# Spectral filter and gated convolution: the two relayouts of a 3200-point transform moved from DRAM passes to 32x32 block transposes

## The chip, the cores and the metric

The kernel runs on one core of one Trainium2 chip. The metric is the device time of one execution in microseconds, as the median of several runs. A profile of one execution is read beside it.

The core has five engines that each work through a queue of their own in order: TensorE (matmuls, PE in the profile, with PEld for loading its stationary operand), VectorE (DVE), ScalarE (ACT), GpSimd (POOL) and SyncE (SP), which here only issues DMAs. Semaphores order the engines among each other.

## The reference

For each of 8 batch elements and 256 channels, a sequence of 3200 samples goes through a real Fourier transform, is multiplied by a complex filter, and goes back. The result feeds a gated unit: a causal convolution of five taps per channel gives the gate, a 256x256 product gives the value, and a second product gives the output.

```python
X = np.fft.rfft(x, axis=1)                    # x: (8, 3200, 256)
Y = X * (filt_r + 1j * filt_i)[None, :, :]
x = np.fft.irfft(Y, n=3200, axis=1).astype(np.float32)
for k in range(5):
    gate_pre += conv_w[k][None, None, :] * xp[:, k:k + S, :]
gate = 1.0 / (1.0 + np.exp(-gate_pre))
return (gate * (x @ w_val)) @ w_out
```

## The kernel before

The transform is split in two stages. A sample index is n = 25 a + r, with a from 0 to 127 and r from 0 to 24 (`L = 128`, `R = 25`). Stage 1 transforms over a, stage 2 over r; the inverse goes the other way. Each stage is a matmul with a table of cosines and sines that the kernel makes at its start.

Every batch element passes through these functions, most of them seven times, one call for each chunk:

- `load_x` (L82): GpSimd issues the load of a chunk of x and its cast to bf16.
- `s1` (L298): stage 1, matmuls of 512 columns with `cf_t`; VectorE copies the PSUM tile to `so` (L310), and SyncE writes it to the DRAM scratch `dscr` (L312).
- `load_t` (L316): SyncE reads `dscr` back as `tt` with another layout (L326), five lines of 25 values to the 125 partitions. This is the first relayout.
- `s2` (L332): stage 2, four matmuls of 256 columns for each of 13 groups (L340 to L346). ScalarE copies PSUM to `xs` (L349); VectorE multiplies by the filter's real part (`za`, L354) and its imaginary part (`zb`, L358) and adds (`z`, L360).
- `inva` (L364): the inverse of stage 2, again four matmuls for each group (L376, L378). ScalarE copies to `u` (L381), and SyncE writes it to the DRAM scratch `escr` (L392).
- `load_v` (L394): SyncE reads `escr` back as `vt`. This is the second relayout.
- `invb` (L403): the inverse of stage 1, with the data as the stationary operand and `ci_t` as the moving one (L413). ScalarE scales it into `yt` (L415), where a row holds one channel and the free dimensions are r and the long index. GpSimd copies four halo rows (L422).
- `conv` (L424): the five taps as 20 matmuls of 64x64 with diagonal tables `dg_t` (L431); ScalarE's sigmoid makes the gate `gt` (L436).
- `val` (L441): four matmuls with `wv_t` (L448); VectorE multiplies the gate with the PSUM tile into `gv` (L453).
- `outp` (L459): eight matmuls with `wo_t` (L465); even chunks are copied to `o` by VectorE (L470), odd ones by ScalarE (L473), and SyncE writes them out (L475).

All PSUM tiles come from one pool of four (L70), each 128 x 1024 float32, and are taken in program order. The order around is written out as one loop over chunk steps (L491), in which each function has a lag in chunks: stage 2 runs nine steps behind stage 1, the inverse of stage 1 ten further. The x loads run seven steps, one batch element, ahead.

Of the kernel before, what the change touches and what calls it, by code (L numbers as in the profile page):

```python
# [11 lines left out]
I32 = mybir.dt.int32  # L12
AF = mybir.ActivationFunctionType
ALU = mybir.AluOpType

PI = math.pi
# [3 lines left out]


L = 128
R = 25
NG = 13
GL = 5
NQ = 2 * NG
P2 = GL * R

PCH = [(0, 4), (4, 4), (8, 4), (12, 3), (15, 3), (18, 3), (21, 4)]
ICH = [PCH[-1]] + PCH[:-1]  # L30
GCH = [(0, 2), (2, 2), (4, 2), (6, 2), (8, 2), (10, 2), (12, 1)]
NCH = 7
# [3 lines left out]
def kernel(  # L36
# [14 lines left out]
    assert D == 256 and S == L * R and K == 5  # L51
# [3 lines left out]
    cf_t = cpool.tile([128, 130], FP16, name="cf_t")  # L55
    ci_t = cpool.tile([128, 128], FP16, name="ci_t")
    wc_t = cpool.tile([128, NG, 128], FP16, name="wc_t")
    ws_t = cpool.tile([128, NG, 128], FP16, name="ws_t")
    wsn_t = cpool.tile([128, NG, 128], FP16, name="wsn_t")
    vc_t = cpool.tile([128, NG, 128], FP16, name="vc_t")  # L60
    vs_t = cpool.tile([128, NG, 128], FP16, name="vs_t")
    vsn_t = cpool.tile([128, NG, 128], FP16, name="vsn_t")
# [5 lines left out]
    b_npi = cpool.tile([128, 1], FP32, name="b_npi")  # L68

    pp = ctx.enter_context(tc.tile_pool(name="ps", bufs=4, space=bass.MemoryType.PSUM))  # L70
    dpool = ctx.enter_context(tc.tile_pool(name="scr", bufs=2, space=bass.MemoryType.DRAM))
    xpool = ctx.enter_context(tc.tile_pool(name="xin", bufs=10))
    spool = ctx.enter_context(tc.tile_pool(name="s1o", bufs=4))
    tpool = ctx.enter_context(tc.tile_pool(name="s2i", bufs=8))
# [4 lines left out]

    xts = {}  # L80

    def load_x(b, j):  # L82
        p0, np_ = PCH[j]
        xt = xpool.tile([128, 4, D], BF16, name="xt")
        src = x[b].rearrange("(a r) d -> a r d", r=R)[:, p0:p0 + np_, :]
        nc.gpsimd.dma_start(out=xt[:, 0:np_, :], in_=src)  # L86
        xts[(b, j)] = xt

    for j in range(NCH):
        load_x(0, j)  # L90


    with tc.tile_pool(name="gen", bufs=1) as g1, \
         tc.tile_pool(name="gen2", bufs=2) as g2, \
         tc.tile_pool(name="genf", bufs=1) as gf:

        def floormod(src_ap, divisor):
            shp = list(src_ap.shape)
            divi = g2.tile(shp, I32, name=f"fm_i{shp[1]}")
            bak = g2.tile(shp, FP32, name=f"fm_b{shp[1]}")  # L100
# [390 lines left out]
    for G in range(total):  # L491
        c = at(G, -NCH)
        if c is not None:
            load_x(*c)
# [57 lines left out]
```

## Time and profile before

| | |
|---|---|
| median of 3 runs | 387.34 us (385.9 to 387.5) |
| the profiled execution, first to last instruction | 385.9 us |
| instructions | 8019 |
| HBM read and written | 56.59 MB and 52.43 MB |
| x loads (GpSimd's queue), share of the 16 DMA engines' time | 28.1% |
| all other transfers (SyncE's queue) | 62.5% |
| first and last start of the convolution's matmuls | 101.3 and 374.8 us |

In the profile's slices, each digit stands for a fortieth of the span and gives the busy share in tenths. The chain of waits follows the work that ended last back to the start and says what it was held by at each step. The groups give, for a line and a shape, the busy time, the mean duration of one instruction, and the idle time of the engine before it with what ended that idle time. The windows give the engines' busy time in a stretch of the execution.

### The profile page before, as it was taken

What the parts mean: (1) busy time and instruction counts of PE and PEld (TensorE: products, weight loads), DVE (VectorE), ACT (ScalarE), POOL (GpSimd) and SP (SyncE); (2) the same over time, 40 slices, a digit from 0 to 9 for tenths busy, and PEclk for the clock granted to TensorE, in tenths of its full rate; (3) what the DMA queues carried; (4) which work ended last, traced back from release to release, by engine and by line L of the source; (5) the groups of instructions that cost most, each with busy time, mean ns of one, the idle gap of its engine ahead of it and who ended that gap; (6) DMA issues with size and microseconds to landing.
All of it is one profiled execution on the core that took longest, in us unless ns stands there. A gap on an engine that the chain in (4) does not pass through costs nothing.

```text
span 385.9 us, 8019 instructions
## 1 busy us (share of the span) xinstructions
PE 312.3 (81%) x3089; PEld 206.9 (54%) x3089; DVE 284.9 (74%) x462; ACT 229.1 (59%) x255; POOL 64.2 (17%) x131
## 2 busy tenths in 40 slices
PE   0230477475899999999997999899999999999992
PEld 0100145253656756766675666566676677666661
DVE  4999958553858887888787789678977677765554
ACT  1100235334976777677765776677677878867660
POOL 8797211112110211021102011100010001001000
PEclk9999998766989999999999999999999999999998
DMA  7999999999999999999999999989595968449343
GB/s 124 144 162 190 216 257 251 231 250 280 179 250 249 311 286 273 263 282 332 274 301 303 286 269 298 285 299 319 201 351 170 304 223 299 136 142 323 141 191 152
DMA packets 94118, 94.53 MB, mean 245 GB/s; under 512 B 10102, under 2 KB 74624, under 8 KB 94080
## 3 DMA queue, kind: packets, MB, share of 16 engines
q1 hardware_dynamic: 80064, 78.98, 62.5%
q0 software_dynamic: 14016, 15.04, 28.1%
q8 instruction: 24, 0.39, 0.4%
q14 instruction: 14, 0.11, 0.1%
HBM read 56.59 MB, written 52.43 MB: 282 GB/s over the span
## 4 chain that ended last, share of the span: by engine, by line
PE 44%; DVE 20%; DMA 19%; SPq 8%; issue 4%; ACT 2%; POOL 1%; DVEq 0%; ACTq 0%; POOLq 0%
PE ps L431 12%; PE ps L448 7%; DMA escr<-u 6%; PE ps L465 6%; DVE so L310 6%; DMA vt<-escr 5%; SPq L326 5%; PE ps L413 5%; DMA dscr<-so 4%; PE ps L376 3%; DVE gv L453 3%; DMA tt<-dscr 3%; PE ps L378 3%; PE ps L307 3%; DVE za L354 2%
## 5 line engine op out<-in xcount | busy, mean ns | idle before, releaser
L415 ACT ACTIVATE yt<-ps 128x1024 bf16<-128x1024 f32 (+1 forms) x56 | 52.1, 931 | 44.3 <-PE ps L413 44.2
L453 DVE TENSOR_TENSOR gv<-ps,gt 128x1024 bf16<-128x1024 f32 (+1 forms) x56 | 61.9, 1104 | 18.7 <-PE ps L448 13.7
L310 DVE CAST so<-ps 128x1024 bf16<-128x1024 f32 (+1 forms) x56 | 61.5, 1103 | 19.0 <-PE ps L307 15.9
L354 DVE TENSOR_TENSOR za<-xs,fr_t 125x1024 bf16<-125x1024 bf16 (+1 forms) x56 | 37.3, 665 | 50.5 <-ACT xs L349 50.3
L381 ACT ACTIVATE u<-ps 125x1024 bf16<-125x1024 f32 (+1 forms) x56 | 53.9, 963 | 24.4 <-PE ps L378 21.6
L431 PE MATMUL ps<-yt,dg_t 64*64 64x512 bf16 (+1 forms) x1120 | 65.7, 361 | 0.8
L349 ACT ACTIVATE xs<-ps 125x1024 bf16<-125x1024 f32 (+1 forms) x56 | 54.0, 965 | 19.6 <-PE ps L346 18.4
L436 ACT ACTIVATE gt<-ps 128x1024 bf16<-128x1024 f32 (+1 forms) x56 | 52.4, 935 | 9.1 <-PE ps L431 5.9
L86 POOL DMA_DIRECT2D xt<-in_x_dram x56 | 30.2, 569 | 153.0 <-PE ps L307 146.5
L307 PE MATMUL ps<-xt,cf_t 128*128 128x512 bf16 x112 | 36.9, 421 | 22.4 <-DVE so L310 11.4
L465 PE MATMUL ps<-wo_t,gv 128*128 128x256 bf16 x400 | 52.8, 273 | 0.9 <-DVE gv L453 0.9
L448 PE MATMUL ps<-yt,wv_t 128*128 128x512 bf16 (+1 forms) x224 | 52.6, 357 | 0.0
L465 PEld LDWEIGHTS <-gv 128*128 128x128 bf16 x400 | 39.1, 98 | 14.9 <-DVE gv L453 1.2
L413 PE MATMUL ps<-ci_t,vt 128*128 128x128 f16 x400 | 31.9, 221 | 13.3 <-DMA vt<-escr 9.6
L431 PEld LDWEIGHTS <-dg_t 64*64 64x64 bf16 x1120 | 30.1, 106 | 23.2 <-issue 10.1
L340 PE MATMUL ps<-tt,wc_t 125*128 125x256 bf16 x104 | 30.1, 289 | 12.9 <-DMA tt<-dscr 10.6
L470 DVE COPY o<-ps 128x1024 f32<-128x1024 f32 (+1 forms) x32 | 36.7, 1148 | 1.1 <-PE ps L465 1.1
L360 DVE TENSOR_TENSOR z<-za,zb 125x1024 bf16<-125x1024 bf16 (+1 forms) x56 | 36.4, 650 | 1.3
L413 PEld LDWEIGHTS <-vt 128*128 128x128 bf16 x400 | 27.0, 98 | 17.9 <-DMA vt<-escr 10.7
L358 DVE TENSOR_TENSOR zb<-xs,fm_t 125x1024 bf16<-125x1024 bf16 (+1 forms) x56 | 36.2, 646 | 0.0
L376 PE MATMUL ps<-z,vc_t 125*128 125x256 bf16 x104 | 30.0, 289 | 6.9 <-DVE z L360 6.9
L307 PEld LDWEIGHTS <-cf_t 128*128 128x128 f16 x112 | 9.2, 108 | 41.7 <-issue 28.2
(109 smaller groups left out, 386.6 us busy)
## 6 DMA issues: line engine op xcount, KB each, us to landing
out_dram<-o SPq DMA_DIRECT2D x32, 512.0 KB
tt<-dscr SPq DMA_DIRECT2D x48, 256.0 KB
escr<-u SPq DMA_DIRECT2D x48, 224.0 KB
out_dram<-o SPq DMA_DIRECT2D x24, 384.0 KB
xt<-in_x_dram POOLq DMA_DIRECT2D x32, 256.0 KB, 6.5
dscr<-so SPq DMA_DIRECT2D x32, 256.0 KB
vt<-escr SPq DMA_DIRECT2D x32, 256.0 KB
xt<-in_x_dram POOLq DMA_DIRECT2D x24, 192.0 KB, 5.7
```

Source lines behind the costliest of these rows:

```text
L307: nc.tensor.matmul(ps[:, a * D:e * D], lhsT=cf_t[:, 0:128], rhs=xt[:, a:e, :], start=True, stop=True)
L310: nc.vector.tensor_copy(so[:, 0:np_, :].rearrange("p a d -> p (a d)"), ps[:, 0:np_ * D])
L349: nc.scalar.activation(xs[0:P2, 0:ng, :, :].rearrange("p g c d -> p (g c d)"), ps[0:P2, 0:ng * 512], AF.Copy)
L354: nc.vector.tensor_tensor(za[0:P2, 0:ng], xs[0:P2, 0:ng], fr_t[0:P2, g0:g0 + ng, :].unsqueeze(2).to_broadcast((P2, ng, 2, D)), op=ALU.mult)
L381: nc.scalar.activation(u[0:P2, 0:2 * ng, :].rearrange("p q d -> p (q d)"), ps[0:P2, 0:ng * 512], AF.Copy)
L413: nc.tensor.matmul(ps[:, o:o + L], lhsT=v[:, a, 128 * dh:128 * dh + 128], rhs=ci_t[:, :], start=True, stop=True)
L415: nc.scalar.activation(y[:, :, H + p0:H + p0 + np_, :].rearrange("p h a n -> p h (a n)"), ps[:, :].rearrange("p (h n) -> p h n", h=2)[:, : ...
L431: nc.tensor.matmul(ps[64 * dh:64 * dh + 64, 512 * r:512 * r + np_ * L], lhsT=dg_t[rows, dh, k, :], rhs=y[rows, dh, p0 + k:p0 + k + np_, :] ...
L436: nc.scalar.activation(g[:, :, 0:np_ * L], ps[:, :].rearrange("p (h n) -> p h n", h=2)[:, :, 0:np_ * L], AF.Sigmoid)
L448: nc.tensor.matmul(ps[:, 512 * eh:512 * eh + np_ * L], lhsT=wv_t[:, dh, 128 * eh:128 * eh + 128], rhs=y[:, dh, H + p0:H + p0 + np_, :], st ...
L453: nc.vector.tensor_tensor(gv[:, :, 0:np_ * L], ps[:, :].rearrange("p (h n) -> p h n", h=2)[:, :, 0:np_ * L], g[:, :, 0:np_ * L], op=ALU.mult)
L465: nc.tensor.matmul(ps[:, D * a:D * a + D], lhsT=gv[:, eh, L * a:L * a + L], rhs=wo_t[:, eh, :], start=(eh == 0), stop=(eh == 1))
```

## The change

The sample index is split differently, n = 32 a + r, with a from 0 to 99 and r from 0 to 31 (`NI = 100`, `NR = 32`). Both relayouts stay in the core. Stage 1's output lies in one large tile `sbig` of a batch element, as 128 channel pairs x 32 values x 2 channels in each partition. VectorE transposes it in blocks of 32x32 words of four bytes, a word being a pair of channels in bf16, into `tbig`. The same is done from `ubig` to `vbig` between the two inverse stages. There are one `sbig`, one `tbig`, one `ubig` and two `vbig`.

```diff
-L = 128
-R = 25
+NI = 100
+NR = 32
-    dpool = ctx.enter_context(tc.tile_pool(name="scr", bufs=2, space=bass.MemoryType.DRAM))
-    xpool = ctx.enter_context(tc.tile_pool(name="xin", bufs=10))
+    xpool = ctx.enter_context(tc.tile_pool(name="xin", bufs=8))
+    sbig = [bigp.tile([128, 128, NR, 2], BF16, name=f"sb{n}") for n in range(1)]
+    tbig = [bigp.tile([128, 128, NR, 2], BF16, name=f"tb{n}") for n in range(1)]
+    ubig = [bigp.tile([128, 128, NR, 2], BF16, name=f"ub{n}") for n in range(1)]
+    vbig = [bigp.tile([128, 128, NR, 2], BF16, name=f"vb{n}") for n in range(2)]
+    def words(t):
+        return t[...].rearrange("p d q l -> p (d q l)").bitcast(U32)
     def s1(b, j):
+        for a in range(2):
+            nc.tensor.matmul(ps[:, 512 * a:512 * a + 512], lhsT=cf_t[0:NI, :],
+                             rhs=xt[0:NI, 2 * a:2 * a + 2, :], start=True, stop=True)
+        nc.scalar.activation(s[:, :, 4 * j:4 * j + 4, :],
+                             ps[:, :].rearrange("p (r d l) -> p d r l", r=4, l=2), AF.Copy)
-        nc.vector.tensor_copy(so[:, 0:np_, :].rearrange("p a d -> p (a d)"),
-                              ps[:, 0:np_ * D])
-        nc.sync.dma_start(
-            out=dscr[0:128 * R, :].rearrange("(i r) d -> i r d", r=R)[:, p0:p0 + np_, :],
-            in_=so[:, 0:np_, :])
+    def tr(dst, src, part):
+        n = 1024
+        nc.vector.transpose(out=words(dst)[:, n * part:n * part + n],
+                            in_=words(src)[:, n * part:n * part + n])
+    def tr1(b):
+        for part in range(4):
+            tr(tbig[b % len(tbig)], sbig[b % len(sbig)], part)
+    def tr2(b):
+        for part in range(4):
+            tr(vbig[b % len(vbig)], ubig[b % len(ubig)], part)
     def s2(b, m):
+            for co in range(2):
+                for h in range(2):
+                    t = 4 * m + 2 * a + h
+                    nc.tensor.matmul(
+                        ps[64 * h:64 * h + 64, 512 * a + D * co:512 * a + D * co + D],
+                        lhsT=wf_t[:, t, co].rearrange("p b k -> p (b k)"),
+                        rhs=tt[:, :, place(t), :], start=True, stop=True)
-        nc.vector.tensor_tensor(z[0:P2, 0:ng], za[0:P2, 0:ng], zb[0:P2, 0:ng],
-                                op=ALU.add)
+        nc.gpsimd.tensor_tensor(za[:, 0:ng], za[:, 0:ng], zb[:, 0:ng], op=ALU.add)
     def inva(b, m):
+            for c in range(2):
+                for h in range(2):
+                    rows = slice(64 * h, 64 * h + 64)
+                    nc.tensor.matmul(
+                        ps[:, 512 * h + D * a:512 * h + D * a + D],
+                        lhsT=wi_t[rows, 2 * m + a, c].rearrange("p b e r -> p (b e r)"),
+                        rhs=z[rows, a, c, :], start=(c == 0), stop=(c == 1))
+            nc.scalar.activation(u[:, :, 4 * m:4 * m + 4, :],
+                                 ps[:, :].rearrange("p (q d l) -> p d q l", q=4, l=2),
+                                 AF.Copy)
     def invb(b, j):
+                nc.tensor.matmul(ps[:, o:o + NI], lhsT=v[:, :, r0 + a, dh],
+                                 rhs=ci_t[:, :], start=True, stop=True)
     def outp(b, c):
-        if j % 2 == 0:
...
+        nc.vector.tensor_copy(o[:, 0:nq, :].rearrange("p a d -> p (a d)"), ps[:, 0:nq * D])
```

`load_t` and `load_v` are gone. Stage 1 has eight chunks for each batch element instead of seven. The convolution, the values and the outputs are cut along the long index: six chunks of 512 columns, which cover 16 values of a for all 32 values of r, and a seventh of 128. The moving operand of the convolution and of the values is then read as 16 neighbouring elements at a time.

The tables are smaller, and their making is rewritten: fewer VectorE instructions, each over 1664 elements, and three sines on ScalarE (`cf_t`, `wf_t` in two halves, `si`), of which `si` follows from `xi`. On VectorE the order that results puts the product of the filter's imaginary part and its sign (`fm_t`, two instructions) between the two halves of `xi`.

The loop over chunk steps is replaced by a list with due times, sorted once; the due times fix the order in which the work is issued:

```diff
+    work = []
+    for b in range(B):
+        for j in range(8):
+            if b + 1 < B:
+                work.append((b + 0.1 * j - 0.05, load_x, (b + 1, j)))
+            work.append((b + 0.1 * j, s1, (b, j)))
+        work.append((b + 0.85, tr1, (b,)))
+        for m in range(NCH):
+            work.append((b + 1.0 + 0.1 * m, s2, (b, m)))
+            work.append((b + 1.15 + 0.1 * m, inva, (b, m)))
+            work.append((b + 2.0 + 0.06 * m, invb, (b, m)))
+            work.append((b + 2.5 + 0.13 * m, conv, (b, m)))
+            work.append((b + 2.57 + 0.13 * m, val, (b, m)))
+            work.append((b + 2.7 + 0.13 * m, outp, (b, m)))
+        work.append((b + 1.9, tr2, (b,)))
+    for _, f, args in sorted(work, key=lambda w: w[0]):
+        f(*args)
```

## The prediction

> **What bounds the kernel now.** I read the busy table, the slices, the chain, then windows of one batch each.
>
> ```profile
> span 385.9 us, 8019 instructions
> PE 312.3 (81%) x3089; PEld 206.9 (54%) x3089; DVE 284.9 (74%) x462; ACT 229.1 (59%) x255; POOL 64.2 (17%) x131
> DMA  7999999999999999999999999989595968449343
> PE 44%; DVE 20%; DMA 19%; SPq 8%; issue 4%; ACT 2%; POOL 1%; DVEq 0%; ACTq 0%; POOLq 0%
> ```
>
> The DMA engines are full until slice 27 (about 260 us). The chain's DMA and SPq shares (27%) are the four DRAM passes, yet most of the chain is TensorE and VectorE. The windows' columns are length, then busy time of PE, PEld, DVE, ACT, POOL, then clock, DMA share and GB/s.
>
> ```profile
> 182.00:223.00 41.00, 37.58 (x390) 25.47 (x388) 32.01 (x41) 28.58 (x32) 5.01 (x10) 1.00 1.02 294
> 305.00:346.00 41.00, 41.00 (x459) 28.30 (x456) 29.54 (x38) 32.01 (x37) 1.29 (x3) 1.00 0.63 206
> ```
>
> In the middle DMA (1.02) and TensorE (37.6 of 41) are both full; later, with DMA down to 0.63, TensorE is busy for all 41 us. In the chain the first convolution of a batch recurs at 106.9, 145.8, 184.7, 225.2 and 265.1 us: a batch takes 39.6 us. So removing DRAM traffic alone gains little: a gain needs TensorE relieved too, and nothing put in its place.
>
> **Durations.** Columns: busy us, mean ns, idle before.
>
> ```profile
> L349 ACT ACTIVATE xs<-ps 125x1024 bf16<-125x1024 f32 x48 | 49.2, 1026 | 19.6 <-PE ps L346 18.4 <-DVE gv L453 0.4
> L453 DVE TENSOR_TENSOR gv<-ps,gt 128x1024 bf16<-128x1024 f32 x32 | 39.0, 1220 | 10.2 <-PE ps L448 5.6 <-ACT gt L436 4.5
> L470 DVE COPY o<-ps 128x1024 f32<-128x1024 f32 x24 | 29.2, 1215 | 1.1 <-PE ps L465 1.1
> L422 POOL COPY yt<-yt 128x508 bf16<-128x508 bf16 x16 | 9.3, 610 | 91.6 <-ACT yt L415 91.6
> L234 DVE TENSOR_SCALAR fm_t<-fi_t,sg 125x3328 bf16<-125x3328 bf16 x1 | 1.9, 1930 | 0.0
> ```
>
> Neighbours overlap, so what an engine pays is the distance between starts; the timeline (start, duration) shows it:
>
> ```profile
> 264.58 1.02 ACT L415 ACTIVATE yt<-ps 128x1024 bf16<-128x1024 f32 x1
> 265.50 0.59 ACT L349 ACTIVATE xs<-ps 125x512 bf16<-125x512 f32 x1
> 273.80 1.22 DVE L310 CAST so<-ps 128x1024 bf16<-128x1024 f32 x1
> 274.93 1.22 DVE L453 TENSOR_TENSOR gv<-ps,gt 128x1024 bf16<-128x1024 f32 x1
> 270.63 1.27 PE L431 MATMUL ps<-yt,dg_t 64*64 64x512 bf16 x20
> 271.84 0.60 PE L307 MATMUL ps<-xt,cf_t 128*128 128x512 bf16 x2
> ```
>
> ScalarE pays 0.92 us for 1024 columns (0.5 for 512, 0.74 for 800), VectorE 1.13 from PSUM and 0.61 for one of za, zb. Twenty 64-row, 64-column matmuls of 512 columns take 1.21 us, against 20 x 0.217 = 4.3 one after another: four tiles run at once.
>
> **The change, part by part (per batch).** *DMA.* The passes dscr, tt, escr and vt go with all SP issues but the output's. Of 94.5 MB some 41 stay, so DMA leaves the bound.
>
> *TensorE.* s1 has 16 matmuls of 512 columns: 3.5 us (2.8 before). s2 and inva keep 52 x 256 columns each, but two halves of the array work in pairs. By the four-tile row the pairs run together: 26 x 0.109 = 2.8 us each instead of 5.7; if not, 5.7. invb 64 x 100 columns at the L413 rate, 0.45 ns a column, about 3; convolution 7.5, val 5.5, outp 5.4. Sum 31 us, 36 without pairing. s2 and invb read every 64th element of a partition; no row here has that, bounded by nothing and by twice their matmul time (+6). I take nothing: TensorE then has 15 us of slack in the period below, which covers it; without that slack it would cost those 6.
>
> *ScalarE.* It gains the eight s1 evictions (8 x 0.92 = 7.4) and loses its three output copies. Per batch: s1 7.4, xs 6.0, u 6.0, y 5.8, gates 5.8: 31 us. s1 and u now scatter runs of eight elements; bounds 0.92 (xs row) and twice that. I take 0.92, the row of the same size.
>
> *VectorE.* It loses the so casts and z adds, takes all output copies, and gains eight transposes of 128x1024 words of four bytes. Bounds for one: 0.6 us (L234 does 3328 elements in 1.93 us, so 1024 in 0.6) and 2.26 (two passes of the copy row). I take 1.13, one pass of it: eight are 9.0 us. With za, zb 8.0, gv 7.1, o 7.1: 31 us. [...]
>
> *GpSimd.* The z add moves there. The copy row's pair takes 1.16 us for 2 x 508 elements, 1.14 ns each for one input; two inputs double it: 2.4 us an add (bounds 1.2 and, as twice that again, 4.8). Seven are about 16 us, and eight x loads of 0.53 us share the queue: 20 us, or 38 at the upper bound, under the period either way. GpSimd also holds VectorE up; here a copy pair meets a za:
>
> ```profile
> 209.07 1.16 POOL L422 COPY yt<-yt 128x508 bf16<-128x508 bf16 x2 [5.81 <-ACT yt L415]
> 209.96 0.82 DVE L354 TENSOR_TENSOR za<-xs,fr_t 125x1024 bf16<-125x1024 bf16 x1 [2.63 <-ACT xs L349]
> ```
>
> That za ends at 210.78, 0.55 us after the copies, and takes 0.82 instead of 0.69. [...]
>
> *Setup.* In the changed order all eight s1 evictions of batch 0 stand behind the activation of si, which needs xi, whose second half stands behind fm_t on VectorE, which needs the last filter load. GpSimd's first 8 loads and index work end near 12 us; 16 filter loads at 0.72 each (17.4 us for 24 before) bring it to 24; landing takes 3.8 (row of fi_t): 27.8. Then fm_t 2 x 1.9, the rest of xi, wrapping and copies 4.3, si 1.6: 37.6. Eight evictions 7.4 and four transposes 4.5: first s2 at 49.5 us (before, the first za is at 48.2).
>
> **The period.** Every transpose needs all 128 channels: tr1 waits for all eight s1 of the next batch, tr2 for all seven u, and with one buffer each the next s2, s1 and invb wait for them. On VectorE the order at the end of a batch is tr1 x3, o, gv, tr1, tr2 x4: 8 x 1.13 + 2 x 1.13 = 11.3 us. Behind it stands invb(0), first in TensorE's queue, and on ScalarE its eviction stands before all others; ScalarE has only two gates meanwhile. Then comes the window from the last transpose to the s1(7) eviction. ScalarE alone needs 0.6 + 28.7 us for it. I walked the four queues through it, each instruction starting at the latest of its queue, its input and its PSUM turn (four, in order). ScalarE loses about 5 us more: it waits 0.9 for xs(1) and 0.6 for y(2) (PSUM turns held by o and gv, which VectorE reaches only after the transposes), 0.6 for gate 0, 0.4 for u(5) (its add), 1.3 for s1(7), the rest in pieces under 0.5. s1(7) ends at 34.1, VectorE starts the transposes at 35.0, the next period at 46.3 us.
>
> The sum: first s2 49.5. Batch 0 through stage 2: 22 evictions 19.4, fill 4.9 (s2, za, zb, add, inva), eight transposes 9.0: 83. Second phase, three gates fewer: 43, so 126. Five full periods 231.5: 357.5. Last stage 2 without s1 and tr1: 46.3 - 7.4 - 4.5 = 34.4: 392. Rest: invb 2.8, eight full chunks at 2.93 (conv 1.19, val and outp 0.87 each), two small at 0.8, last gv, outp, copy and DMA 5.6 (before, the DMA took 4.5): 34. Total **426 us**, on the profile's terms; that execution's span of 385.9 lies 0.4% under the median 387.34 of runs 385.9 to 387.5, so nothing is added.
>
> **Rivals.** A, the forecast: two transposes at each batch's end that nothing covers, a period of 46.3; own range 405 to 450. For it: the dependence is structural and the buffers single. Against it: the walk rests on rows of other operations.
>
> B, not slower: ScalarE runs back to back in the window, because evictions free PSUM before TensorE asks. Place: last transpose to s1(7). Price: period 0.6 + 28.7 + 11.3 + 0.1 = 40.7, 5.6 less in some 7.2 periods, so 426 - 40 = 386 us; transposes below 1.13 take it under the time before. It decides below 40.9. For it: in the old window 305:346 TensorE kept 41 of 41. Against it: ScalarE was busy 32 of 41 there.
>
> C, slower still: scattered evictions cost more. Fifteen a batch; each 0.1 us more is 1.5 per period, 11 in all. At 0.3 more, 459 us. It decides from 0.2. Against it: the runs are as wide as a copy needs; no row tells.
>
> D, transposes in two passes: 8 x 1.13 more per period, about 7.8 periods: 426 + 70 = 496 us.
>
> **Chances and range.** A 0.50, B 0.26, C 0.16, D 0.08. About 0.5% is what a measurement of this kernel can tell from no change. B gives 0.22 for faster and 0.04 for same; 0.02 of A's and C's neighbourhood goes to same as well: faster 0.22, same 0.06, slower 0.72. The range must reach B's middle and most of C and D: 376 to 488.
>
> **What would show it.** Right: a transpose row near 1.1 to 1.2 us; ScalarE idle 8 to 10 us per batch until y(0), released through transposes; DMA share under 0.6; s2 and inva at half their time; a period of 45 to 48; first transposes near 45 us. Wrong: a period near 40 with ScalarE over 85% busy (B); s1 and u rows above 1.2 us (C); a transpose near 2.3 us (D); s2 pairs in series, which would put TensorE at 36 us and lengthen the window.

## The result, and the profile after

The changed kernel takes **476.36 us** (median of 3 runs, 474.74 to 477.2) against 387.34 before: 1.232 times the time before, 95% interval 1.225 to 1.239. The forecast was 426. The profiled execution has a span of 473.0 us, 3.4 under the median.

From its page, the lines that answer to those shown of before: the span, the busy table, the slices of TensorE, of its clock and of the DMA engines, and the chain by engine.

```profile
span 473.0 us, 7824 instructions
...
PE 346.1 (73%) x3218; PEld 186.6 (39%) x3218; DVE 294.7 (62%) x346; ACT 268.8 (57%) x294; POOL 179.3 (38%) x206
...
PE   0004356288969994999499949995999779769991
...
PEclk9999997589979999999999999998799989899997
DMA  7864342223434563546354544554222323224454
...
PE 42%; DVE 26%; POOL 10%; ACT 9%; issue 7%; DMA 3%; DVEq 0%; POOLq 0%; ACTq 0%
```

The transfers are gone as announced: behind the first three slices the DMA row lies at 2 to 6, where it held 9s before, and SP's queue leaves the chain. But TensorE's row is not full either. It shows 9s and then a 4 or 5, once a batch. TensorE is busy for 34 us longer than before (346.1 against 312.3), although two of its stages were to run at half their time.

One period in the middle, from one batch's last transpose to the next one's. The columns are those of the windows of before:

```profile
283.50:331.60 48.10, 41.73 (x402) 22.81 (x402) 32.69 (x37) 32.31 (x36) 19.57 (x18) 0.93 0.51 103
```

TensorE 41.7 of 48.1 us, VectorE 32.7, ScalarE 32.3, GpSimd 19.6. The forecast had TensorE at 31, VectorE and ScalarE at 31 each and GpSimd at 20. Three of the four lie within 2 us of it; TensorE is 11 us off. The groups (busy us, mean ns of one, then the idle time before them and its releaser) show where:

```profile
L299 POOL TENSOR_TENSOR za<-za,zb 128x1024 bf16<-128x1024 bf16 (+1 forms) x56 | 111.9, 1998 | 78.7 <-DVE zb L297 77.9
...
L260 ACT ACTIVATE sb<-ps 128x1024 bf16<-128x1024 f32 x64 | 65.1, 1033 | 10.0 <-PE ps L258 5.8
L334 PEld LDWEIGHTS <-vb 128*128 128x128 bf16 x512 | 52.0, 205 | 45.8 <-DVE vb L265 34.1
...
L284 PE MATMUL ps<-tb,wf_t 128*64 128x256 bf16 x416 | 59.0, 416 | 8.6 <-DVE tb L265 7.5
...
L316 ACT ACTIVATE ub<-ps 128x1024 bf16<-128x1024 f32 x48 | 49.4, 1029 | 13.7 <-PE ps L311 13.6
...
L392 PEld LDWEIGHTS <-gv 128*128 128x128 bf16 x400 | 36.4, 99 | 39.6 <-DVE gv L380 29.0
...
L265 DVE STREAM_TRANSPOSE tb<-sb 128x1024 uint32<-128x1024 uint32 x32 | 37.6, 1217 | 10.3 <-ACT sb L260 10.2
```

Loading 128 x 128 weights takes 205 ns where they come from `vbig` and 99 where they come from `gv`. The scattered evictions of ScalarE (L260, L316) cost 1.03 us, no more than the plain ones of before (1026 ns). A transpose costs 1.22 us.

The timeline at the end of a batch (start, duration, and in brackets the idle time before and its releaser):

```profile
272.07 3.50 DVE L265 STREAM_TRANSPOSE tb<-sb 128x1024 uint32<-128x1024 uint32 x3
...
275.49 1.19 DVE L395 COPY o<-ps 128x1024 f32<-128x1024 f32 x1
...
276.60 1.21 DVE L380 TENSOR_TENSOR gv<-ps,gt 128x1024 bf16<-128x1024 f32 x1
277.73 1.22 DVE L265 STREAM_TRANSPOSE tb<-sb 128x1024 uint32<-128x1024 uint32 x1
...
277.87 1.05 PE L392 MATMUL ps<-wo_t,gv 128*128 128x256 bf16 x8 [2.22 <-DVE gv L380]
...
278.75 1.04 PE L375 MATMUL ps<-yt,wv_t 128*128 128x512 bf16 x4
278.88 4.58 DVE L265 STREAM_TRANSPOSE vb<-ub 128x1024 uint32<-128x1024 uint32 x4
283.38 1.18 DVE L395 COPY o<-ps 128x1024 f32<-128x1024 f32 x1
...
283.52 0.95 PE L334 MATMUL ps<-ci_t,vb 128*128 128x100 f16 x8 [3.72 <-DVE vb L265]
...
284.49 1.21 DVE L380 TENSOR_TENSOR gv<-ps,gt 128x1024 bf16<-128x1024 f32 x1
284.57 0.84 ACT L336 ACTIVATE yt<-ps 128x800 bf16<-128x800 f32 x1 [7.84 <-PE ps L334]
```

This is the block that the forecast described: from 272.07 to 283.46 us VectorE has eight transposes, one o copy and one gv. TensorE still finds work in the first part of it, then waits 2.2 and 3.7 us, and ScalarE waits 7.8 us for the first `yt`.

With the ends of the tr2 blocks as marks, the sum of the forecast stands against the trace like this:

| stretch | forecast | measured | off by |
|---|---|---|---|
| to the end of the first tr1 | 49.5 | 55.4 | +5.9 |
| first phase, to the first tr2's end | 33.5 | 39.6 | +6.1 |
| second phase | 43 | 43.0 | 0 |
| five periods | 231.5 (46.3 each) | 242.8 (48.55) | +11.3 |
| last stage-2 phase | 34.4 | 44.9 | +10.5 |
| rest | 34 | 47.2 | +13.2 |
| sum | 426 | 473.0 | +47.0 |

Three of these stretches can be read in single lines. ScalarE at the start, the table `si` and then the eight s1 evictions:

```profile
37.63 1.59 ACT L173 ACTIVATE si<-xi 128x1664 f16<-128x1664 f32 x1 [16.79 <-DVE xi L86]
43.33 7.44 ACT L260 ACTIVATE sb<-ps 128x1024 bf16<-128x1024 f32 x8 [4.10 <-DVE dg_t L226]
```

The eight evictions take 7.44 us as forecast, but they begin 4.1 us after `si` ends. `sbig` lies in the memory in which the tables were made, so the first write into it waits for VectorE's last table instruction, a `dg_t`. `si` itself is 1.6 us late: it ends at 39.2 us and not at 37.6, because `fm_t` starts on VectorE at 29.55 us and not at 27.8. The loads of `fi_t` took 5.5 us to land in this profile, where the forecast had 3.8.

In the first phase, on TensorE, VectorE and GpSimd:

```profile
74.78 0.69 DVE L297 TENSOR_TENSOR zb<-xs,fm_t 128x1024 bf16<-128x1024 bf16 x1
...
76.66 0.55 POOL L70 DMA_DIRECT2D xt<-in_x_dram  x1 [1.87 <-PE ps L258]
...
77.05 2.87 DVE L293 TENSOR_TENSOR za<-xs,fr_t 128x1024 bf16<-128x1024 bf16 x1 [1.58 <-ACT xs L289]
77.23 2.13 POOL L299 TENSOR_TENSOR za<-za,zb 128x1024 bf16<-128x1024 bf16 x1
79.41 1.03 PE L311 MATMUL ps<-za,wi_t 64*128 64x256 bf16 x8 [3.04 <-POOL za L299]
```

The zb of one chunk ends at 75.47, but its add starts only at 77.23: a load of x stands ahead of it in GpSimd's queue and waits for s1. Then the next chunk's za, which needs 0.69 us alone, takes 2.87 and ends 0.56 us after the add. TensorE waits 3.04 us for the add.

In the rest, when only gating and output are left:

```profile
451.81 1.05 PE L392 MATMUL ps<-wo_t,gv 128*128 128x256 bf16 x8 [0.32 <-DVE gv L380]
...
452.69 1.05 PE L375 MATMUL ps<-yt,wv_t 128*128 128x512 bf16 x4
452.89 1.23 DVE L395 COPY o<-ps 128x1024 f32<-128x1024 f32 x1 [1.14 <-PE ps L392]
...
454.03 1.21 DVE L380 TENSOR_TENSOR gv<-ps,gt 128x1024 bf16<-128x1024 f32 x1
...
455.30 1.05 PE L392 MATMUL ps<-wo_t,gv 128*128 128x256 bf16 x8 [0.31 <-DVE gv L380]
```

From one outp to the next it takes 3.49 us. outp ends, o is copied, gv follows on the same engine, and the next outp waits for it. The forecast had added TensorE's three pieces, 2.93.

### The profile page after: what moved, and what is told of

It is laid out like the page before. It is cut to its first block, busy times and chain, and to the rows that moved or that the text cites. A ratio compares the mean times of both kernels' runs of the same rounds, so it can differ in the third digit from the quotient of the medians.

```text
span 473.0 us, 7824 instructions
## 1 busy us (share of the span) xinstructions
PE 346.1 (73%) x3218; PEld 186.6 (39%) x3218; DVE 294.7 (62%) x346; ACT 268.8 (57%) x294; POOL 179.3 (38%) x206
## 4 chain that ended last, share of the span: by engine, by line
PE 42%; DVE 26%; POOL 10%; ACT 9%; issue 7%; DMA 3%; DVEq 0%; POOLq 0%; ACTq 0%
PE ps L284 8%; PE ps L334 8%; PE ps L357 7%; DVE vb L265 7%; PE ps L392 6%; POOL za L299 6%; DVE tb L265 5%; DVE gv L380 4%; DVE o L395 4%; PE ps L311 4%; PE ps L375 4%; PE ps L258 4%; ACT ub L316 3%; ACT xs L289 2%; ACT sb L260 2%
## 5 line engine op out<-in xcount | busy, mean ns | idle before, releaser
L299 POOL TENSOR_TENSOR za<-za,zb 128x1024 bf16<-128x1024 bf16 (+1 forms) x56 | 111.9, 1998 | 78.7 <-DVE zb L297 77.9
L336 ACT ACTIVATE yt<-ps 128x1000 bf16<-128x1000 f32 (+1 forms) x56 | 52.7, 941 | 71.7 <-PE ps L334 71.7
L293 DVE TENSOR_TENSOR za<-xs,fr_t 128x1024 bf16<-128x1024 bf16 (+1 forms) x56 | 47.5, 847 | 72.8 <-ACT xs L289 72.2
L395 DVE COPY o<-ps 128x1024 f32<-128x1024 f32 (+1 forms) x56 | 61.5, 1099 | 48.9 <-PE ps L392 48.9
L334 PE MATMUL ps<-ci_t,vb 128*128 128x100 f16 x512 | 55.4, 257 | 30.6 <-DVE vb L265 29.8
L260 ACT ACTIVATE sb<-ps 128x1024 bf16<-128x1024 f32 x64 | 65.1, 1033 | 10.0 <-PE ps L258 5.8
L334 PEld LDWEIGHTS <-vb 128*128 128x128 bf16 x512 | 52.0, 205 | 45.8 <-DVE vb L265 34.1
L289 ACT ACTIVATE xs<-ps 128x1024 bf16<-128x1024 f32 (+1 forms) x56 | 54.4, 971 | 23.8 <-PE ps L284 19.0
L284 PE MATMUL ps<-tb,wf_t 128*64 128x256 bf16 x416 | 59.0, 416 | 8.6 <-DVE tb L265 7.5
L316 ACT ACTIVATE ub<-ps 128x1024 bf16<-128x1024 f32 x48 | 49.4, 1029 | 13.7 <-PE ps L311 13.6
L392 PEld LDWEIGHTS <-gv 128*128 128x128 bf16 x400 | 36.4, 99 | 39.6 <-DVE gv L380 29.0
L258 PE MATMUL ps<-xt,cf_t 100*128 100x512 bf16 x128 | 46.8, 460 | 6.3 <-ACT sb L260 4.9
L265 DVE STREAM_TRANSPOSE tb<-sb 128x1024 uint32<-128x1024 uint32 x32 | 37.6, 1217 | 10.3 <-ACT sb L260 10.2
```

Of the source, the lines that this page charges most:

```text
L258: nc.tensor.matmul(ps[:, 512 * a:512 * a + 512], lhsT=cf_t[0:NI, :], rhs=xt[0:NI, 2 * a:2 * a + 2, :], start=True, stop=True)
L260: nc.scalar.activation(s[:, :, 4 * j:4 * j + 4, :], ps[:, :].rearrange("p (r d l) -> p d r l", r=4, l=2), AF.Copy)
L265: nc.vector.transpose(out=words(dst)[:, n * part:n * part + n], in_=words(src)[:, n * part:n * part + n])
L284: nc.tensor.matmul(ps[64 * h:64 * h + 64, 512 * a + D * co:512 * a + D * co + D], lhsT=wf_t[:, t, co].rearrange("p b k -> p (b k)"), rhs=t ...
L289: nc.scalar.activation(xs[:, 0:ng].rearrange("p g c d -> p (g c d)"), ps[:, 0:ng * 512], AF.Copy)
L299: nc.gpsimd.tensor_tensor(za[:, 0:ng], za[:, 0:ng], zb[:, 0:ng], op=ALU.add)
```

## The experiments

The kernel before, run beside each group, took 384.2 to 387.7 us. "Period" is the mean distance between the starts of tr2 from the second batch to the seventh.

### What the spread reads cost

**e1.** Stage 2 reads 256 neighbours instead of every 32nd word; the values are others.

```diff
-                        rhs=tt[:, :, place(t), :], start=True, stop=True)
+                        rhs=flat(tt)[:, 256 * t:256 * t + 256], start=True, stop=True)
```

> Stage 2 (s2) reads 256 neighbouring elements of tbig in place of every 64th word, so it transforms other values; all else is the changed kernel. Theory (TensorE bounds the window after the transposes because s2 reads single words 128 bytes apart): eight s2 matmuls fall from 1.0 us to 0.45 to 0.6, the period from 48.5 to about 45, the time from 476 to about 450. Rival 1 (the 64-column halves don't run in pairs): eight stay at 0.87 or more, the time above 465. Rival 2 (PSUM turns and ScalarE set the window): eight fall, but the time stays above 470.

Measured 463.95 us (ratio 1.201, 1.194 to 1.209), period 47.3. The group of stage 2:

```profile
L287 PE MATMUL ps<-tb,wf_t 128*64 128x256 bf16 x416 | 39.7, 317 | 5.2 <-DVE tb L268 4.0
```

It was 59.0 and 416. Eight matmuls now follow each other within 0.56 us instead of 1.0; one after another, at the forecast's 0.109 each, they would take 0.87. So with neighbours the two halves of the array do run in pairs, and reading 4 bytes of every 128 takes all of that gain away. The whole fell by less than expected: 12 of the 26 us.

**e2.** The same for the weights of invb; the values are others.

```diff
-                nc.tensor.matmul(ps[:, o:o + NI], lhsT=v[:, :, r0 + a, dh],
+                nc.tensor.matmul(ps[:, o:o + NI], lhsT=flat(v)[:, 128 * (2 * (r0 + a) + dh):128 * (2 * (r0 + a) + dh) + 128],
```

> invb loads as its stationary operand 128 neighbouring elements of vbig in place of every 64th element, so it transforms other values; all else is the changed kernel. Theory (spread stationary loads bound invb): the loads fall from 205 ns to about 100, ten matmuls from 1.0 us to about 0.5, the period by 3 us, the time from 476 to about 452. Rival (invb's ten matmuls lie beside other work): the loads fall, the time stays above 468.

Measured 469.3 us (1.215, 1.208 to 1.222), period 47.8.

```profile
L337 PEld LDWEIGHTS <-vb 128*128 128x128 bf16 x512 | 30.0, 108 | 49.2 <-DVE vb L268 34.8
```

The load falls from 205 to 108 ns, yet the time by 7 us only: the total agrees with the rival.

**e5.** Both together (the values are others).

> Both reads as neighbouring elements at once (stage 2's moving and invb's stationary operand), so other values; else the changed kernel. Theory (my walk was right but for these two prices): the window from the last transpose to the next is the walk's 35 us or less, the period 46.5 instead of 48.5, and the time is the sum of the two single savings, 12 and 7 us: 455 to 459. Rival (the two hide each other, and once both are gone TensorE is no longer what the window waits for): below 450.

Measured 453.49 us (1.179, 1.164 to 1.194), period 46.0: between the range of the theory and that of the rival. The two are worth 22.9 us together and 12.4 and 7.1 apart. The forecast's walk had 46.3, but that the two agree is in part luck: TensorE is still busy for some 37 us of a period here, and not for the forecast's 31.

**e3.** The other way to neighbours: the transposes write r by r, so s2 finds neighbours and invb every second element, and the transposes scatter their output in words 512 bytes apart.

```diff
+        by_r = dst[...].rearrange("p q d l -> p q (d l)").bitcast(U32)
-        nc.vector.transpose(out=words(dst)[:, n * part:n * part + n],
+        nc.vector.transpose(out=by_r.rearrange("p q d -> p d q")[:, 32 * part:32 * part + 32],
...
-                        rhs=tt[:, :, place(t), :], start=True, stop=True)
+                        rhs=tt[:, place(t), :, :], start=True, stop=True)
...
-                nc.tensor.matmul(ps[:, o:o + NI], lhsT=v[:, :, r0 + a, dh],
+                nc.tensor.matmul(ps[:, o:o + NI], lhsT=v[:, r0 + a, :, dh],
```

> The transposes write tbig and vbig with r outside and the channel inside, so that s2 reads 256 neighbouring elements and invb every second element; the result is the reference's. Theory: both savings together, TensorE from 41.5 to about 35 us of a period, period 42 to 43, time 420 to 430; the transposes stay at 1.15 us apart. Rival 1: a transpose that scatters its output costs more than 1.3 us, and takes the saving back. Rival 2 (the window is set by others): above 460.

Measured 498.12 us (1.289, 1.283 to 1.296), period 51.1.

```profile
L266 DVE STREAM_TRANSPOSE tb<-sb 128x1024 uint32<-128x1024 uint32 x32 | 58.4, 1907 | 10.2 <-ACT sb L260 10.2
```

A transpose now takes 1.9 us instead of 1.2. Eight of them lie in the block, and the period grows by 2.6 us: VectorE pays more there than TensorE gains, as the first rival had it. The kernel's choice of layout was the cheaper one.

### What the transposes cost

**e4.** The transposes are left out: stage 2 reads `sbig` and invb what inva wrote, in two buffers each; the values are others.

```diff
...
-        work.append((b + 0.85, tr1, (b,)))
...
-        work.append((b + 1.9, tr2, (b,)))
```

> Leaves both transposes out: s2 reads what s1 wrote and invb what inva wrote, from two buffers each, with the same spread reads; the values are then others. Theory (the block of eight transposes, 11.4 us with what lies among them, is covered by nothing): the period falls from 48.5 to TensorE's own 41.5 to 42.5, the time to 405 to 425. Rival (TensorE's backlog would have filled that time anyway): above 450.

Measured 417.87 us (1.082, 1.076 to 1.088), period 41.7 (here and in e9, which have no tr2, between the starts of invb). TensorE's slices:

```profile
PE   0003655778999999999999999999999997899981
```

58 us go with the transposes and their waits, and TensorE becomes full. How much of it is owed to the second buffers, which take waits away as well, this run does not tell. Even so the kernel is 8% above the one before: what TensorE does in a batch is by itself more than the 39.6 us of before.

**e9.** Both: no transposes and no spread reads.

> The eight transposes of a batch are left out (the matmuls read what the first stages wrote, in two buffers each), and stage 2 and the second inverse stage read 256 and 128 neighbours, so the values are others. Theory: transposes without cover and spread reads are all that holds the changed kernel above the one before. From e4 (417.9 us, 41 us a batch, TensorE full) the reads take off 0.44 x 7 for s2 and 0.45 x 7 for invb, 6 us a batch in some 7 batches: 375 to 388 us, a period of 35 to 37 with TensorE still full. Rival: ScalarE (31 us a batch plus its waits) or GpSimd's add take over at once: 395 us or more, TensorE idle over 10% in the middle.

Measured 396.21 us (1.030, 1.020 to 1.040), period 38.2, TensorE busy for 44.4 of 48 us in the middle. That is 1 us over the rival's bound and 8 over the theory, though TensorE is idle for 8% there and not for 10. Of the 92 us that the changed kernel stands above the one before in this group (384.74), 80 are held by the transposes, with their single buffers, and the spread reads together; the last 11 are not. They do not lie in the middle, where 38.2 us is less than the 39.6 of before. The convolutions of the first and of the sixth batch begin at 102.0 and 294.0 us in e9 and at 101.3 and 297.8 in the kernel before; from the sixth to the last batch e9 then takes 67.2 us, and the kernel before 58.0.

### The start and the first phase

**e13.** `sbig` gets memory of its own.

```diff
+    sbig = [cpool.tile([128, 128, NR, 2], BF16, name="sb0")]
-    sbig = [bigp.tile([128, 128, NR, 2], BF16, name=f"sb{n}") for n in range(1)]
```

> The buffer that the first stage writes gets memory of its own instead of the memory in which the tables were made. Theory: 4 of the 5.9 us that the start came late are s1's first eviction waiting until 43.3 us for VectorE's last table instruction; it then starts when si is done, tr1 of the first batch ends at 51 to 52 instead of 55.4, nothing behind it changes and the whole falls to 471 to 474 us. Rival: ScalarE's own table work or the x tiles hold it as long, tr1 ends after 54 and the whole stays above 475.

Measured 470.39 us (1.220, 1.204 to 1.236). The first tr1 on VectorE:

```profile
44.70 4.62 DVE L265 STREAM_TRANSPOSE tb<-sb 128x1024 uint32<-128x1024 uint32 x4 [1.78 <-ACT sb L260]
```

It ends at 49.3; the forecast had 49.5 and the expectation 51 to 52. The wait is gone, but it was 4.1 us, and tr1 ends 6.1 earlier. ScalarE shows the difference:

```profile
35.63 2.85 ACT L260 ACTIVATE sb<-ps 128x1024 bf16<-128x1024 f32 x3 [14.80 <-PE ps L258]
38.51 1.59 ACT L174 ACTIVATE si<-xi 128x1664 f16<-128x1664 f32 x1
40.00 4.66 ACT L260 ACTIVATE sb<-ps 128x1024 bf16<-128x1024 f32 x5
```

With memory of its own three of the eight evictions run ahead of `si`, where the forecast had all eight behind it, as they are in the changed kernel. So e13 shows the wait, but lands on the forecast's number by luck. The period stays at 48.6.

**e6.** The z add goes back to VectorE.

```diff
-        nc.gpsimd.tensor_tensor(za[:, 0:ng], za[:, 0:ng], zb[:, 0:ng], op=ALU.add)
+        nc.vector.tensor_tensor(za[:, 0:ng], za[:, 0:ng], zb[:, 0:ng], op=ALU.add)
```

> The z add goes back to VectorE (all else the changed kernel, the result is the reference's). Theory (GpSimd's 2.1 us add and the x loads queued before it hold the inverse stage 2): the phase before the first inverse stage 1 falls from 39.6 us by 6 to 10, the steady period by 1 or less, since VectorE pays 0.6 for each add: time 462 to 470. Rival (VectorE is the fuller engine): 480 or more.

Measured 460.1 us (1.196, 1.181 to 1.211), 2 us under the theory's range. The first phase is 29.8 us instead of 39.6; the period 48.1, as good as unchanged. The last stage-2 phase falls as well, from 44.9 to 41.3 us. On GpSimd the add costs next to nothing in the middle; with the loads that stand ahead of it, it costs 10 us at the beginning and some 3.6 in the last stage-2 phase.

**e10 and e16** were to take away the wait of the x loads ahead of the adds.

```diff
-                work.append((b + 0.1 * j - 0.05, load_x, (b + 1, j)))
+                work.append((b + 0.1 * j + 0.45, load_x, (b + 1, j)))
```

> Each load of the next batch's x is issued half a batch later, when the tile that it fills is already free. Theory: in the first phase the loads wait on GpSimd for TensorE's s1 and hold up the adds queued behind them; without that wait the time from the first batch's last tr1 (55) to its last tr2 falls from 39.6 to 30 to 34 us, and the whole to 466 to 471 us; the five middle periods stay at 48.5. Rival: the adds are slow by themselves (2.14 us each against 1.3 of the pair on VectorE), the phase stays above 37 and the whole above 473.

Measured 476.23 us, first phase 39.3. This tells nothing about the loads: in the two traces every engine's queue is the same, instruction by instruction, so the later due time moved nothing. It is a second measurement of the changed kernel. The medians lie 0.1 us apart, but its period is 48.9 and not 48.55, so differences of 0.4 us in a period mean nothing.

```diff
-    xpool = ctx.enter_context(tc.tile_pool(name="xin", bufs=8))
+    xpool = ctx.enter_context(tc.tile_pool(name="xin", bufs=16))
-    vbig = [bigp.tile([128, 128, NR, 2], BF16, name=f"vb{n}") for n in range(2)]
+    vbig = [bigp.tile([128, 128, NR, 2], BF16, name=f"vb{n}") for n in range(1)]
```

> Sixteen x tiles instead of eight (and one vbig instead of two, to make room), so a load no longer waits on GpSimd for s1 to free its tile. Theory: the waits of 2.8, 0.5, 1.9 and 0.4 us ahead of the loads in the first phase go, and the adds behind them come earlier: the phase between the first batch's last tr1 and its last tr2 falls from 39.6 to 33 to 36 us, the middle periods stay at 48 to 49. Rival: the phase is set by the adds themselves, one after the other with VectorE and TensorE between them: above 37.5.

Measured 476.66 us, first phase 39.7. The loads waited 2.8, 0.6, 2.0 and 0.4 us as before: with sixteen tiles they are issued a batch earlier and wait for s1 again. The wait was not removed, so the run decides nothing.

**e17.** The loads themselves are left out: all batches read the x of batch 0, so the values are others.

> Every batch reads the x tiles of batch 0, loaded once; the loads of the other seven batches are left out, so the values are those of batch 0 eight times. Theory: the loads, queued on GpSimd ahead of adds that are ready and waiting themselves for s1, are what stretches the first phase; from the trace they hold two adds by 2.8 and 1.9 us and set the two that follow against a za or zb: the phase falls from 39.6 to 32 to 36 us, the middle periods stay within 1 us of 48.5. Rival: the add itself does it, 2.13 us on GpSimd in the place of 0.61 on VectorE seven times, and shuts out za and zb whatever the loads do: the phase stays above 37 us.

Measured 473.28 us (1.230, 1.220 to 1.240); first phase 35.5, period 48.9. Both causes are real. The loads are worth 4.1 us of the first phase; the 5.7 us from 35.5 down to e6's 29.8 are the add's own price on GpSimd.

### The block and the clock

**e7.** invb, conv, val and outp are due 0.3 of a batch later, so that some of them stand ahead of the transposes' end.

```diff
-            work.append((b + 2.0 + 0.06 * m, invb, (b, m)))
...
+            work.append((b + 2.30 + 0.06 * m, invb, (b, m)))
...
```

> Due times alone: invb, conv, val and outp 0.3 of a period later, so that s2 and s1 of the next batch stand ahead of invb in TensorE's queue and run during tr2. Theory (the block costs because invb stands first): 4 to 5 us of the block are covered, TensorE idles once for 3 us less and keeps its clock, period 44 to 45, one third of a period more at the end: 450 to 462. Rival (za and zb, which stand behind tr2 on VectorE, are what the rest waits for): above 470.

Measured 459.23 us (1.194, 1.178 to 1.211), period 46.6: the whole in its range, the period 2 us above what was expected of it.

**e8.** In addition tr2's four parts are spread between the multiplications of stage 2 (two `ubig`, one `vbig`).

```diff
...
-        work.append((b + 1.9, tr2, (b,)))
+        for part in range(4):
+            work.append((b + 1.92 + 0.1 * part, tr2, (b, part)))
```

> As the run with invb later, and the four parts of tr2 get due times 0.1 apart, with two ubig and one vbig (the same memory). Theory: only tr1 stays as a block, period 42 to 43, near TensorE's own 40 to 41.5; time 435 to 450. Rival (single buffers of tbig and vbig hold the next batch): no better than the run with due times alone.

Measured 447.39 us (1.163, 1.143 to 1.183), period 44.3, where 42 to 43 was expected. The end of a batch there, on TensorE:

```profile
209.07 1.32 PE L356 MATMUL ps<-yt,dg_t 64*64 64x512 bf16 x20
213.49 1.89 PE L391 MATMUL ps<-wo_t,gv 128*128 128x256 bf16 x8 [3.10 <-DVE gv L379]
215.17 1.91 PE L374 MATMUL ps<-yt,wv_t 128*128 128x512 bf16 x4
...
221.96 1.04 PE L391 MATMUL ps<-wo_t,gv 128*128 128x256 bf16 x8
222.83 1.04 PE L374 MATMUL ps<-yt,wv_t 128*128 128x512 bf16 x4
```

Only tr1 lies open now. After the idle 3.1 us the same eight and four matmuls take 1.89 and 1.91 us instead of 1.04: TensorE's granted clock is 0.50 from 212.64 to 219.47 us, and 1.00 in the 88 us before and the 83 us after. It does not fall each time. One batch earlier, at 169.44, outp took 1.05 us after 3.06 idle us. In the changed kernel it falls at every block from the second batch on, to 0.50 for 3.41 us (from 234.97 and from 282.76, for example) and once for 10.24; a convolution at 382.76, 1.8 us behind an idle stretch of 3.73, took 2.35 us instead of 1.31.

The stretches at half clock in the middle last 3.41 us, 6.83 (the one in e8) or 10.24. In e8 the clock fell 2.3 us behind the end of the last matmul (210.39), in a gap of 3.1 us; why it did not fall one batch earlier, in a gap of nearly the same length, these traces do not show.

**e11.** 14 matmuls without use fill the idle stretch ahead of invb.

```diff
+        for i in range(14 if j == 0 else 0):
+            nc.tensor.matmul(ps[:, 512 * (i % 2):512 * (i % 2) + 512], lhsT=wv_t[:, 0, 0:128], rhs=fr_t[:, 0:2, :], start=True, stop=True)
```

> Ahead of each batch's first invb matmul, 14 matmuls of 128x512 on constant tiles go into the same PSUM tile, which invb then overwrites: about 3.0 us of work without use in the 3.7 us in which TensorE has nothing. Theory: the clock falls because of that idle stretch, and its price lies behind it; with the stretch filled the clock of the middle periods goes from 0.93 to 0.98 or more, the period from 48.5 to 46 to 47, the whole to 458 to 468 us. Rival 1: the clock rises, but ScalarE's chain sets the window, so the whole stays within 4 us of 476. Rival 2: the clock falls for another reason and stays under 0.95.

Measured 471.37 us (1.225, 1.212 to 1.238), period 47.8, clock 0.96 to 1.00 in the middle.

```profile
275.96 3.23 PE L332 MATMUL ps<-fr_t,wv_t 128*128 128x512 bf16 x14
...
279.88 0.91 PE L338 MATMUL ps<-ci_t,vb 128*128 128x100 f16 x8
```

The clock stays up, and 0.8 us a period comes of it, of which e10's scatter could be half: between the theory and the first rival. So the clock is a small part of the miss in the periods. At the ends it counts for more: the second phase falls from 43.0 to 40.7 us and the last stage-2 phase from 44.9 to 41.8. The rest, in which the fill only adds to TensorE, grew from 47.2 to 52 us.

### The rest after the last transpose

**e12.** The last batch's output copies go to ScalarE.

> The last batch's output copies go to ScalarE. Theory: in the rest after the last tr2 each chunk costs 3.5 us because VectorE runs o copy and gv one after the other while TensorE waits; with the copy on ScalarE a chunk is TensorE's conv, val and outp, 3.0 us, and the rest falls from 47.2 to 43 to 45 us: 472 to 474 in the whole. Rival: ScalarE's gates and copies queue in the same way and the chunk stays at 3.4 or more: 475 or more.

Measured 476.81 us (1.239, 1.231 to 1.248), a rest of 47.6: no gain, as the rival had it.

```profile
458.42 1.05 PE L392 MATMUL ps<-wo_t,gv 128*128 128x256 bf16 x8
459.30 1.05 PE L375 MATMUL ps<-yt,wv_t 128*128 128x512 bf16 x4
...
460.28 1.31 PE L357 MATMUL ps<-yt,dg_t 64*64 64x512 bf16 x20
460.46 1.23 DVE L380 TENSOR_TENSOR gv<-ps,gt 128x1024 bf16<-128x1024 f32 x1 [2.10 <-PE ps L375]
...
461.74 1.05 PE L392 MATMUL ps<-wo_t,gv 128*128 128x256 bf16 x8
```

A chunk takes 3.32 us, between the theory's 3.0 and the rival's 3.4, and the copy is no longer in its way. By these lines it is a loop: gv can start only when val is done, val stands behind the outp before, and the next outp waits for gv: 0.88 + 1.16 + 1.28. The convolution is all that fills it.

### Together

**e14.** e8, `sbig` in memory of its own, and batch 0's adds on VectorE.

```diff
+        adder = nc.vector if b == 0 else nc.gpsimd
-        nc.gpsimd.tensor_tensor(za[:, 0:ng], za[:, 0:ng], zb[:, 0:ng], op=ALU.add)
+        adder.tensor_tensor(za[:, 0:ng], za[:, 0:ng], zb[:, 0:ng], op=ALU.add)
```

> e8 (447.4 us) with the buffer of e13 in memory of its own and batch 0's z adds on VectorE. Theory: the two act on stretches of their own, 4 us at the start and 7 to 9 us in the first phase, and the period stays at 44.4: 434 to 440 us. Rival: the first phase of e8 is already set by something else, and it stays at 443 or more.

Measured **432.6 us** (430.5 to 433.2; ratio 1.121, 1.112 to 1.130), period 44.5: 1.4 us better than expected. The terms add up. Of the versions that leave nothing out it is the best, and it is still slower than the kernel before.

**e15 and e18** place the transposes' outputs as in e3 within e14, e15 for both relayouts, e18 for the second alone.

> e14 with the transposes' outputs placed as in e3, so that stage 2 and the second inverse stage read neighbours. Theory: with tr2 spread, only tr1 lies open; its four transposes grow from 4.6 to 7.1 us, but TensorE, full elsewhere at 40 us a batch, loses 5.6: period 41 to 43, the whole 12 to 22 us under e14. Rival: VectorE, at 37 us of work and with 7.1 us blocks, becomes the limit, and the whole is at e14's time or over it, as e3 was over the changed kernel.

Measured 446.34 us (1.158, 1.147 to 1.169), period 46.0. The rival held: TensorE was busy for some 35 us of 43, but tr1's block took 7.1 us, in which TensorE stood idle for up to 5.4.

> e14 with only the second transposes' outputs placed as in e3: they are spread under other work, so their growth (1.15 to 1.77 us apart) should be covered, while the loads of the second inverse stage's weights fall from 0.92 to 0.45 us per ten. Theory: TensorE, 40 us of e14's period of 44.6, loses 2.5 to 3 us and the period falls to 42 to 43: 416 to 425 us. Rival: VectorE's 2.5 us more end in the chain through gv that feeds TensorE, and the whole stays at 432 or rises.

Measured 436.6 us (1.134, 1.127 to 1.142), period 44.8. Here too the rival's number came. TensorE's busy time falls from some 41 us of a period to some 39, and the period does not follow. That VectorE's longer tr2 reaches TensorE through gv is argued, not shown; what limits e18 stays open.

## Why the prediction was off

Of the four cases A, the forecast, comes nearest, but the time lies outside its own range of 405 to 450, and the period outside 45 to 48. One half of its mechanism is right. The two transposes at a batch's end make a block of 11.4 us (11.3 forecast), a transpose is 1.15 us from start to start (1.13), and ScalarE waits 7.8 us for the first `yt` (8 to 10). The second phase comes to 43.0 us (43), though partly by luck, since the clock falls in it: with the fill of e11 it is 40.7. Rivals B, C and D fall: no period near 40, scattered evictions at 1.03 us, a transpose at 1.15 us and not 2.26. The other half is wrong: between two blocks TensorE sets the pace, and not ScalarE. Beside it several terms were too small.

**TensorE in the period.** The failing step is this: "s2 and invb read every 64th element of a partition; ... I take nothing: TensorE then has 15 us of slack in the period below, which covers it". The upper bound of 6 us was right in size: seven times 0.44 for s2 and seven times 0.47 for invb are 6.4. That slack covered it was wrong. The 15 us were counted over the whole period. In the window from the last transpose of one block to the first of the next, TensorE has almost none; the columns are as before, the first line is of the changed kernel, the second of e5:

```profile
235.01:272.07 37.06, 35.96 (x354) 20.16 (x358) 21.28 (x27) 29.84 (x34) 19.59 (x18) 0.95 0.51 100
225.17:259.30 34.13, 31.10 (x354) 17.20 (x358) 21.68 (x27) 29.63 (x34) 19.41 (x18) 0.95 0.56 109
```

TensorE is busy for 36.0 of 37.1 us, ScalarE for 29.8; the forecast had a window of 35.0, set by ScalarE. With neighbouring reads (e5) TensorE is down to 31.1 of 34.1 us and the period to 46.0. So of the 6.4 us some 2.6 come through in each period. Of e5's gain 13 us lie in the five periods, 3.4 in the first phase and 3.1 in the last stage-2 phase. The forecast's own sign for this case came as well: eight s2 matmuls at 1.0 us are slower than the 0.87 of pairs in series. A sum per engine says whether an engine is the bound of a period; it does not say that its delays are hidden in the stretch where it has to do its work.

The rest of the 11 us on TensorE are partly pieces that the forecast had too short without those reads: convolution 8.0 against 7.5, inva 3.5 against 2.8, s1 4.0 against 3.5, val 6.0 against 5.5, by the distances in the trace, with the clock at 0.93 to 0.97. That makes 2.2 us; some 2 more are not accounted for.

**The start, +5.9.** The sum followed `si` on ScalarE and missed that `sbig` takes the place of the tables' scratch memory, so that s1's output also waits for the last instruction that uses it: 4.1 us, which e13 removes. Another 1.6 are `si` itself, which ends later by the landing of the filter's loads. The evictions and transposes took what the forecast had, to 0.2 us.

**The first phase, +6.1.** The forecast showed one za that took 0.82 us instead of 0.69 beside GpSimd's copies, and its sum has no term for a za or zb that meets an add. In the middle next to none is needed: in the window shown, none of the twelve full-sized za and zb meets an add, and none takes longer than 0.69 us; the full-sized o copies and gv that an add overlaps take 1.22 to 1.23 us, as elsewhere (1.18 to 1.23). In the first phase there are no gv and no o yet, and three of twelve took 2.1 to 2.9 us instead of 0.68, 5.6 us in all. Each of the three ends 0.55 us after the add that it met. That is 1.9 us a meeting, not much less than a whole add (2.13 us). To this come the loads that stand ahead of the adds and wait for s1 (4.1 us, e17). The forecast had counted them on GpSimd at their own 0.53 us, not with what they wait for. With the adds off GpSimd the phase is 29.8 us (e6), under the forecast's 33.5: an error of the other sign hides 3.7 us of these 9.8.

**The last stage-2 phase, +10.5.** The forecast took ScalarE's work off a period. TensorE, busy for 38.6 of these 44.9 us, was the longer one, with two convolutions at 2.35 us and two waits for adds (2.15 and 1.51) on top. The runs made for other questions bear this out one by one: the phase is 41.3 us with the adds on VectorE (e6), 41.8 with the clock kept up (e11) and 41.8 with neighbouring reads (e5).

**The rest, +13.2.** The chunk's loop at 3.49 us instead of 2.93 over the last batch's chunks, and one chunk more than counted, make some 6 us; the time from the end of the last copy to the end is 7.2 us, where 4.5 were taken for that transfer. The other 4 to 5 lie in the first 19 us, where the convolutions, val and outp of the batch before share TensorE with the last invb. invb's spread weights are not what costs there: with neighbouring weights the rest is still 46.9 (e2) and 46.7 us (e5). e12 shows that the copy behind which gv stood is not the cause of the long loop either, since the loop itself is almost as long.

The parts overlap, so the experiments' gains must not be added to the 47.

That the change makes this kernel slower even without its two largest costs is settled: with transposes and spread reads taken away (e9) it comes to 1.03 times the time before. Not settled is why e9 loses those 3% over the last batches, and what limits e18.

## What to carry to other kernels

A relayout that needs a whole batch's data makes a block on its engine; price the block with everything queued behind it, and spread its parts under other work before anything else, which gave back 29 of 89 us here, 17 of them by the order of issue alone (e7). When a transposing instruction dictates a layout, price its readers too, and count their engine's slack in the stretch where they run, not over the whole period. A small instruction moved to another queue is priced with what its queue neighbours wait for, and in the phases at both ends, where the cover of the middle is missing.

## What the runs showed of the hardware that was not expected

- A matmul that reads 4 bytes of every 128 of a partition: eight of 256 columns, in two halves of the array, 1.0 us instead of 0.56. Weights read as 2 bytes of every 128: 205 ns instead of 108.
- A transpose of 128 x 1024 words takes 1.22 us with neighbouring output and 1.9 with output words 512 bytes apart. ScalarE's scattering in runs of eight elements costs nothing (1.03 us; the plain evictions of before 1026 ns).
- A za on VectorE that meets a GpSimd add takes up to 2.87 us instead of 0.69, and ends 0.56 us after the add.
- After 3.1 us of idling, TensorE ran the same matmuls in 1.89 us or in 1.05, one batch apart. Its granted clock fell to 0.50 for 3.41, 6.83 or 10.24 us at a time in the middle.
